# Attention before a feed-forward block: the small products put into 64x64 tiles of the array

## The chip, the core and the metric

One core of a Trainium2 chip runs the whole program. The metric is the device time of one execution in microseconds (us), and the median over several executions is compared. TensorE (PE) does the matrix products and has a separate record for its weight loads (PEld); VectorE (DVE), ScalarE (ACT) and GpSimd (POOL) do the rest; the SyncE queue (SP) issues all transfers.

## The reference, cut to what matters

```
attn:  B, H, S, D = 8, 8, 576, 64     scores = q k^T / 8
       heads 0..3 (local):    key allowed where 0 <= query - key < 32
       heads 4..7 (strided):  key allowed where key <= query and key % 32 == query % 32
       softmax over the allowed keys, times v
x = attn_out as (B*S, H*D) = (4608, 512)
h = x @ w_in                          (512 -> 2048)
out = (h * sigmoid(1.702 h)) @ w_out  (2048 -> 512)
```

All inputs and the output are float32.

## The kernel before, in words

The 4608 tokens go through the feed-forward part (FFN) in 12 groups of G = 384. A group takes 16 steps, one for each 128 columns of the hidden layer. A step does 12 products into the bank `h` (`ffn1`), the activation (`act`), and two steps later (LAG = 2) 9 products into three output banks `o` (`ffn2`). These products are of float32r tiles: each operand is kept as a high and a low part and three of the four cross products are added. A float32r product shows as one matmul record.

The attention is cut into units, listed by `_pairs()`; `p` numbers them. A unit always holds two query blocks (U = 2) of four heads, thus eight score matrices (HU = 8). A local unit has two blocks of 96 queries by 128 keys (QL, KL; 32 keys lie before the block). A strided unit has two blocks in which 6 or 5 of the 32 residues are laid one behind the other: 108 or 90 queries by as many keys (RES), of which only the blocks of 18 by 18 on the diagonal are allowed. There are 24 local and 24 strided units.

For a unit, `scores` computes the eight matrices in plain float32, which the trace shows as two matmul records for each product. Head dimension 64 fills half the rows of the array, and two heads lie on the two halves of the partitions (index j), so their products use rows 0 to 63 and 64 to 127 and write two banks. `maxima` adds the mask and finds the row maxima (DVE), `softmax` does eight exponentials with sums (ACT), two small DVE operations and a scaling on POOL, `transpose` turns the probabilities in 32x32 blocks (DVE), and `values` multiplies by v: the stationary operand is 64 columns of v, the outputs of the two heads go to partitions 0 to 63 and 64 to 127 of one bank `a`. ACT and DVE then split the result into the high and low parts of the FFN's input (`xh..`, `xl..`).

The first n0 units (10 before) are done ahead of the FFN in a loop of their own (line 559). There the mask is added by a bf16 product into the score bank, the probabilities are turned on TensorE (`turn_pr`, tile `t`) and fetched by DVE (`fetch_pt`). One pass of that loop issues, in this order: the scores of unit i+1, the transfer of q and k for unit i+3, the scaling of unit i-1, the exponentials of unit i, the products with v of unit i-2, the load of v for unit i, a weight load, and one beat of the weights' preparation (`weigh`: rebuilding float32 from two words and splitting it, on ACT and DVE; three beats make one of 16 weight tiles). The remaining 38 units are spread over the FFN steps: `due` gives the step in which a unit's probabilities are turned; in the step after it, its products with v and the scores of a unit two later are put between `ffn1` and `ffn2` (lines 641 to 650). The order of the TensorE instructions is kept as written.

Of the kernel before, what the change touches and what calls it, by code (L numbers as in the profile page):

```python
# [9 lines left out]
F32 = mybir.dt.float32  # L10
# [64 lines left out]
def attn_ffn(ctx, tc, qk, vs, w_in, w_out, masks, ident, out):  # L75
# [48 lines left out]
    def load_qk(p):  # L124
        if p < len(pairs) and p not in qks:
            qks[p] = st4([P, 2, 2, U, P], F32, f"qk_{p}")
            for g in (slice(0, 1), slice(1, 2)) if p == 0 else (slice(0, 2),):
                sync.dma_start(out=qks[p][:, :, g], in_=qk[p][:, :, g])

    def load_v(p):  # L130
        if p < len(pairs) and p not in vts:
            vts[p] = io.tile([P, U, HEADS, D], F32, tag="v", name=f"v_{p}", bufs=2)
            sync.dma_start(out=vts[p], in_=vs[p])

# [4 lines left out]
    masks_sb = const.tile([P, 4, P], BF16, name="masks_sb")  # L139
# [12 lines left out]
    prs = [const.tile([P, HU, P], F32, name=f"pr_{i}") for i in range(AHEAD)]  # L152
    pts = {
        "l": const.tile([P, HU, QL], F32, name="pt_l"),
        "s": const.tile([P, HU, P], F32, name="pt_s"),
    }
# [3 lines left out]
    def geom(p):  # L160

        kind, b, c = pairs[p]
        if kind == "l" and c == 0:
            m = masks_sb[:QL, 0:U].rearrange("p u n -> p (u n)")
            return QL, KL, m.unsqueeze(1).broadcast_to([QL, 2, U * KL])
        n, nk, i = (QL, KL, 1) if kind == "l" else (RES[c] * NPOS, RES[c] * NPOS, 2)
        return n, nk, masks_sb[:n, i, :nk].unsqueeze(1).broadcast_to([n, 2 * U, nk])

    def scores(p):

        nq, nk, mask = geom(p)
        t = qks[p]
# [3 lines left out]
        if onto:  # L176
            for sp in sps:
                matmul(
                    sp[:nq, : 2 * U * nk].rearrange("p (a n) -> p a n", a=n),
                    lhsT=masks_sb[:nq, 3, :nq], rhs=mask, start=True, stop=False,  # L180
                )
# [12 lines left out]
        banks[p] = sps  # L194

    def maxima(p):


        nq, nk, mask = geom(p)
        sps, pr, n = banks.pop(p), prs[p % AHEAD], mask.shape[1]  # L200
        nmax = nmaxs[p] = small.tile([P, HU], F32, tag="nmax", name=f"nmax_{p}")
        if p < n0:
            for j in range(2):
                vector.tensor_reduce(
                    out=nmax[:nq, j * 2 * U : (j + 1) * 2 * U],
                    in_=sps[j][:nq, : 2 * U * nk].rearrange("p (h n) -> p h n", n=nk),
                    axis=AX.X, op=ALU.max, negate=True,
                )
            vector.tensor_scalar_mul(out=nmax[:nq], in0=nmax[:nq], scalar1=SCALE)
            exps[p] = [  # L210
                (sps[i // (2 * U)][:nq, i % (2 * U) * nk : (i % (2 * U) + 1) * nk], SCALE)
# [3 lines left out]
        for j in range(2):  # L215
            o = pr[:nq, j * 2 * U : (j + 1) * 2 * U, :nk]
            if n == 2:
                o = o.rearrange("p (g u) n -> p g (u n)", g=2)
            vector.scalar_tensor_tensor(
                out=o, in0=sps[j][:nq, : 2 * U * nk].rearrange("p (a n) -> p a n", a=n),  # L220
# [3 lines left out]
            out=nmax[:nq], in_=pr[:nq, :, :nk], axis=AX.X, op=ALU.max, negate=True  # L224
        )
        exps[p] = [(pr[:nq, i, :nk], 1.0) for i in range(HU)]

    def softmax(p):

        nq, nk, _ = geom(p)  # L230
        nmax, pr = nmaxs.pop(p), prs[p % AHEAD]
        ssum = small.tile([P, HU], F32, tag="ssum", name=f"ssum_{p}")
        for i, (x, scale) in enumerate(exps.pop(p)):
            scalar.activation(
                pr[:nq, i, :nk], x, AF.Exp,
                bias=nmax[:nq, i : i + 1], scale=scale,
                accum_out=ssum[:nq, i : i + 1],
# [4 lines left out]
        vector.tensor_scalar_add(out=rinv[:nq], in0=ssum[:nq], scalar1=1e-9)  # L242
        vector.reciprocal(out=rinv[:nq], in_=rinv[:nq])
        gpsimd.tensor_tensor(
            out=pr[:nq, :, :nk],
            in0=pr[:nq, :, :nk],
            in1=rinv[:nq].unsqueeze(2).broadcast_to([nq, HU, nk]),
# [3 lines left out]
    def transpose(p):  # L251


        nq, nk, _ = geom(p)
        kind, pr = pairs[p][0], prs[p % AHEAD]
        pt = pts[kind]
        for qb in range(-(-nq // BL)):
            for kb in (qb, qb + 1) if kind == "l" else range(max(qb - 1, 0), qb + 1):
                i, o = slice(qb * BL, (qb + 1) * BL), slice(kb * BL, (kb + 1) * BL)
                vector.transpose(out=pt[o, :, i], in_=pr[i, :, o])  # L260

    def turn_pr(p):

        nq, nk, _ = geom(p)
        for i in range(HU):
            n = i % (2 * U)
            transposed(
                first[2][i // (2 * U)][:nk, n * nq : (n + 1) * nq], prs[p % AHEAD][:nq, i, :nk],
                ident_sb[:nq, :nq],
            )  # L270

    def fetch_pt(p):
        nq, nk, _ = geom(p)
        for j, t in enumerate(first[2]):
            vector.tensor_copy(
                out=pts[pairs[p][0]][:nk, j * 2 * U : (j + 1) * 2 * U, :nq],
                in_=t[:nk, : 2 * U * nq].rearrange("p (h n) -> p h n", h=2 * U),
            )
# [4 lines left out]
    def part(kind, j):  # L283
        if (kind, j) not in xs:
            xs[kind, j] = [
                xp.tile([P, 2, G], F32R, tag=f"x{s}_{kind}", name=f"x{s}{kind}_{j}",
                        bufs=2 if kind == "l" else 3)
# [4 lines left out]
    def values(p):  # L292

        kind, b, c = pairs[p]
        nq, nk, _ = geom(p)
        v, pt = vts[p], pts[kind]
        ops = first_a[p % 2 if p < n0 - 3 else 0] if p < n0 else bank(f"a_{p}")
        for u in range(U):
            for g in range(2):
                for j in range(2):  # L300
                    i = g * U + u
                    matmul(
                        ops[j * D : (j + 1) * D, i * nq : (i + 1) * nq],
                        lhsT=v[:nk, u, 2 * g + j, :],
                        rhs=pt[:nk, j * 2 * U + i, :nq],
                        start=True,
                        stop=True,
                    )
        parts = []
        if kind == "l":  # L310
            j, o = divmod((NL * b + c) * QL, G)
            src = ops[:, : 2 * U * nq].rearrange("p (g n) -> p g n", g=2)
            parts.append([src] + [x[:, :, o : o + U * QL] for x in part("l", j)])
        else:
            n, r0 = U * RES[c], R0[c]
            src = ops[:, : 2 * U * nq].rearrange("p (g r t) -> p g t r", g=2, r=n)
            t0 = 0
            while t0 < NPOS:
# [4 lines left out]
                    [src[:, :, t0:t1]] + [x[:, :, o : o + t1 - t0, r0 : r0 + n] for x in xv]  # L323
# [335 lines left out]
def _layout(q, k, v, w_in, w_out):  # L659
    hl = H // 2  # L660
    pad = np.zeros((B, hl, STRIDE, D), np.float32)
    kp, vp = (np.concatenate([pad, x[:, :hl]], axis=2) for x in (k, v))

    def strided(x, b, c):
        y = x[b, hl:].reshape(hl, NPOS, STRIDE, D)[:, :, R0[c] : R0[c] + RES[c]]
        return y.transpose(0, 2, 1, 3).reshape(hl, RES[c] * NPOS, D)

    pairs = _pairs()[0]

    qk = np.zeros((len(pairs), 2, D, 2, 2, U, P), np.float32)  # L670
    vs = np.zeros((len(pairs), P, U, HEADS, D), np.float32)
    for p, (kind, b, c0) in enumerate(pairs):
        for u in range(U):
            c = c0 + u
            if kind == "l":
                i = slice(c * QL, (c + 1) * QL)
                j = slice(c * QL, c * QL + KL)
                x = [q[b, :hl, i], kp[b, :, j], vp[b, :, j]]
            else:
                x = [strided(y, b, c) for y in (q, k, v)]  # L680
            vs[p, : x[2].shape[1], u] = x[2].transpose(1, 0, 2)
            for e, y in enumerate(x[:2]):
                n = y.shape[1]
                qk[p, :, :, e, :, u, :n] = y.reshape(2, 2, n, D).transpose(1, 3, 0, 2)
    qk = qk.reshape(len(pairs), P, 2, 2, U, P)

# [4 lines left out]
    return qk, vs, wi, wo  # L691


def _masks():
    import ml_dtypes

    m = np.full((P, 4, P), NEG, ml_dtypes.bfloat16)
    qi, ki = np.arange(QL)[:, None], np.arange(KL)[None, :] - STRIDE
    rel = qi - ki
    ok = (rel >= 0) & (rel < STRIDE)  # L700
    m[:QL, 0][ok & (ki >= 0)] = 0.0
    m[:QL, 1][ok] = 0.0
    i = np.arange(QS)
    ok = (i[:, None] // NPOS == i[None, :] // NPOS) & (i[:, None] >= i[None, :])
    m[:QS, 2, :QS][ok] = 0.0
    m[:, 3] = np.eye(P)
# [27 lines left out]
```

## Time and profile before

| | |
|---|---|
| median of 3 runs | 938.94 us (938.4 to 941.64) |
| profiled execution | 940.96 us, of which its span is 939.2 us |
| granted TensorE clock, mean of the span | 0.993 of 2.4 GHz |
| PE busy | 924.2 us in 5674 matmul records |
| DVE, ACT, POOL busy | 520.5, 407.7, 85.7 us |

The span runs from the first to the last instruction of the program on the core; 1.76 us of the profiled execution lie around it. A busy time is a sum of records, and records of TensorE overlap, so the share of an engine says only whether it ever pauses. What a piece of work costs on TensorE is better read from the starts of successive records: the time from the start of one block to the start of the next. The line number is L108 throughout, because a helper there records every operation; pieces are told apart by the names of their tiles (`s`, `u` scores; `t` turned probabilities; `a` products with v; `h`, `o` FFN).

### The profile page before, as it was taken

To read this page: it belongs to the slowest core of one execution; us is meant where nothing else is said; L and a number is where in the kernel's file an instruction comes from. 1 tells how busy PE (TensorE), PEld (TensorE's weight loads), DVE (VectorE), ACT (ScalarE), POOL (GpSimd) and SP (SyncE) were. 2 spreads that over 40 slices of the span, in tenths; PEclk is the share of its full clock that TensorE was granted. 3 is DMA by queue.
4 is the path that set the end of the run, shared out by engine and by line. 5 is a ranking of instruction groups with operands and counts; after the bars stand their busy time and mean duration, and the time that the engine had idled before them with its cause. 6 is when DMAs were issued, how large, how long until landed. Compare 5 with 4: busy or idle time off the path is not lost.

```text
span 939.2 us, 14695 instructions
## 1 busy us (share of the span) xinstructions
PE 924.2 (98%) x5674; PEld 813.2 (87%) x5674; DVE 520.5 (55%) x1000; ACT 407.7 (43%) x1289; POOL 85.7 (9%) x56
## 2 busy tenths in 40 slices
PE   8799999999999999999999999999999999999998
PEld 5589888888888888888888888898888888888997
DVE  4787564676666554626757665544656655422322
ACT  6997563434344443325343443333344444222221
POOL 3310000011001100101010100000010101000000
PEclk7999999999999999999999999999999999999999
DMA  7894020222122111103212121102211210000000
GB/s 268 304 343 171 1 90 28 75 68 68 51 75 57 56 35 67 35 0 102 57 45 81 55 68 45 36 21 68 65 37 56 80 46 12 34 1 1 34 1 34
DMA packets 24373, 65.10 MB, mean 69 GB/s; under 512 B 2672, under 2 KB 3440, under 8 KB 24304
## 3 DMA queue, kind: packets, MB, share of 16 engines
q1 hardware_dynamic: 24304, 64.17, 20.3%
q8 instruction: 44, 0.72, 0.3%
q14 instruction: 25, 0.20, 0.1%
HBM read 54.72 MB, written 9.44 MB: 68 GB/s over the span
## 4 chain that ended last, share of the span: by engine, by line
PE 95%; DMA 2%; DVE 1%; ACT 1%; issue 0%; SPq 0%; ACTq 0%
PE o L108 44%; PE h L108 43%; PE s L108 4%; PE a L108 4%; DMA qk<-qk 2%; ACT pr L108 1%; PE u L108 1%; PE t L108 0%; DVE w L108 0%; SPq L108 0%; ACT raw L108 0%; DVE raw L108 0%; DVE nmax L108 0%; DVE pt_l L108 0%; DVE pt_s L108 0%
## 5 line engine op out<-in xcount | busy, mean ns | idle before, releaser
L108 PE MATMUL o<-w,gh 128*128 128x512 f32 x1152 | 308.0, 398 | 0.0
L108 PEld LDWEIGHTS o<-w,gh 128*128 128x128 f32 x1152 | 210.9, 187 | 40.3
L108 PE MATMUL h<-xhl,w 128*128 128x384 f32 x768 | 229.1, 339 | 0.4 <-DVE w L108 0.4
L108 PE MATMUL h<-xhs,w 128*128 128x384 f32 x768 | 226.6, 335 | 0.0
L108 DVE SCALAR_TENSOR_TENSOR g<-g,h 128x384 f32<-128x384 f32 x192 | 106.4, 554 | 194.6 <-ACT g L108 193.7
L108 ACT ACTIVATE g<-h 128x384 f32<-128x384 f32 x192 | 93.5, 487 | 245.0 <-PE h L108 177.5
L108 PE MATMUL o<-w,gl 128*128 128x512 f32 x576 | 169.5, 395 | 0.0
L108 DVE TENSOR_TENSOR gl<-g,gh 128x384 fp32r<-128x384 f32 x192 | 125.9, 656 | 73.5 <-ACT gh L108 72.8
L108 ACT ACTIVATE pr<-pr,nmax 96x128 f32<-96x128 f32 (+2 forms) x304 | 114.2, 378 | 113.1 <-DVE nmax L108 109.6
L108 ACT CAST gh<-g 128x384 fp32r<-128x384 f32 x192 | 98.8, 514 | 130.4 <-DVE g L108 130.1
L108 PEld LDWEIGHTS h<-xhl,w 128*128 128x128 f32 x768 | 141.9, 188 | 9.5 <-DVE w L108 0.7
L108 POOL TENSOR_TENSOR pr<-pr,rinv 96x1024 f32<-96x1024 f32 (+2 forms) x48 | 82.1, 1710 | 707.1 <-DVE rinv L108 630.7
L108 PEld LDWEIGHTS h<-xhs,w 128*128 128x128 f32 x768 | 141.4, 188 | 0.1
L108 PEld LDWEIGHTS o<-w,gl 128*128 128x128 f32 x576 | 107.9, 187 | 26.5
L108 PE MATMUL h<-xll,w 128*128 128x384 f32 x384 | 129.4, 337 | 0.0
L108 PE MATMUL h<-xls,w 128*128 128x384 f32 x384 | 128.3, 334 | 0.0
L108 PEld LDWEIGHTS h<-xll,w 128*128 128x128 f32 x384 | 72.1, 188 | 8.7
L108 PEld LDWEIGHTS h<-xls,w 128*128 128x128 f32 x384 | 72.1, 188 | 0.0
L108 DVE TENSOR_SCALAR rinv<-ssum 96x8 f32<-96x8 f32 (+2 forms) x48 | 8.0, 167 | 96.2 <-ACT pr L108 96.2
L108 ACT ACTIVATION_READ_ACCUMULATOR pr<-pr,nmax 96x1 f32 (+2 forms) x304 | 57.1, 188 | 0.0
L108 DVE STREAM_TRANSPOSE pt_l<-pr 32x256 f32<-32x256 f32 x120 | 52.1, 434 | 3.7 <-POOL pr L108 2.3
L108 PEld LDWEIGHTS s<-qk 64*96 64x96 f32 (+2 forms) x688 | 37.4, 166 | 9.8 <-issue 3.3
(55 smaller groups left out, 555.7 us busy)
## 6 DMA issues: line engine op xcount, KB each, us to landing
qk<-qk SPq DMA_DIRECT2D x47, 512.0 KB, 4.1
v<-vs SPq DMA_DIRECT2D x48, 256.0 KB, 2.8
out<-out SPq DMA_DIRECT2D x36, 256.0 KB, 2.3
raw<-w_in SPq DMA_DIRECT2D x16, 512.0 KB, 5.4
raw<-w_out SPq DMA_DIRECT2D x16, 512.0 KB, 6.3
qk<-qk SPq DMA_DIRECT2D x2, 256.0 KB, 3.3
masks_sb<-masks SPq DMA_DIRECT2D x1, 128.0 KB, 2.2
ident_sb<-ident SPq DMA_DIRECT2D x1, 64.0 KB, 5.1
```

The costliest lines, as they stand in the source:

```text
L108: ins = call(*args, **kw)
```

## The change

Local units become four blocks of 64 queries by 96 keys (QB, KB). Blocks are numbered u and g; block g = 0 goes to output partitions 0 to 63 and g = 1 to 64 to 127, so that one unit covers 256 tokens. There are 18 local units instead of 24. `scores` does 16 products for a unit instead of 8, each with 64 stationary columns; with the head on the rows (j) and the block on the columns (g), four successive products use the four 64x64 quarters of the array. Local `values` does 16 products of 64 columns instead of 8 of 96.

Strided units hold 12 residue places in four blocks of 3 (NB = 54 queries by 54 keys), used as 12, 10 and 10. Their scores are 16 products of 64 stationary columns (10 of them padding) by 54 keys. Their products with v stay 8 for a unit, with both blocks of a pair in one block-diagonal matrix of 118 rows and 108 columns. The number of strided units stays 24.

The units of the loop ahead of the FFN become 9 (2 local, 3 strided, then strided, local, strided, strided); 15 local and 18 strided units are spread over the FFN steps instead of 20 and 18. Every group of rows has all 128 partitions now; the free sizes of scores, exponentials and scaling become 96 (local) and 54 (strided) for each of eight matrices instead of 128 and 108 or 90. Transposes on DVE are 8 for a local unit (6 before) and 6 for a strided one (7 or 5 before). A local unit's q and k take 576 KB and its v 384 KB, a strided unit's 452 KB and 236 KB (512 KB and 256 KB for all units before). The input tiles of the local part have three buffers instead of two, since a unit can reach into the next group. The masks and the host's layout follow the new shapes.

```diff
-QL = 96
-KL = 128
-NL = S // QL
-RES = (6, 6, 5, 5, 5, 5)
-R0 = (0, 6, 12, 17, 22, 27)
-QS = 6 * NPOS
+QB = 64
+KB = QB + STRIDE
+RB = 3
+NB = RB * NPOS
 U = 2
+LT = U * 2 * QB
+NP = B * S // LT
+RES = 4 * RB
+NR = (12, 10, 10)
+R0 = (0, 12, 22)
+QW = (U * 2 * QB, U * (NB + QB))
+KW = (U * (KB + QB), U * 2 * NB)
+QKW = tuple(2 * (a + b) for a, b in zip(QW, KW))
...
     def strided(b):
-        return [("s", b, c) for c in range(0, len(RES), U)]
+        return [("s", b, c) for c in range(len(NR))]
 
     def local(j):
-        n = G // QL
-        return [("l", i // NL, i % NL) for i in range(j * n, (j + 1) * n, U)]
+        return [("l", i, 0) for i in range(-(-j * G // LT), -(-(j + 1) * G // LT))]
...
     def load_qk(p):
         if p < len(pairs) and p not in qks:
-            qks[p] = st4([P, 2, 2, U, P], F32, f"qk_{p}")
-            for g in (slice(0, 1), slice(1, 2)) if p == 0 else (slice(0, 2),):
-                sync.dma_start(out=qks[p][:, :, g], in_=qk[p][:, :, g])
+            kind, a, c = pairs[p]
+            src, n = (lqk[a], QKW[0]) if kind == "l" else (sqk[a * len(NR) + c], QKW[1])
+            qks[p] = st4([P, QKW[0]], F32, f"qk_{p}")
+            for i in (slice(0, n // 2), slice(n // 2, n)) if p == 0 else (slice(0, n),):
+                sync.dma_start(out=qks[p][:, i], in_=src[:, i])
...
+    def operands(p, rows, h, u, g):
+
+        x, kind = qks[p], pairs[p][0] == "s"
+        base = h * QKW[kind] // 2
+        q = base + u * QW[kind] // U + g * (QB, NB)[kind]
+        k = base + QW[kind] + u * KW[kind] // U + g * (QB, NB)[kind]
+        return x[rows, q : q + QB], x[rows, k : k + (KB, NB)[kind]]
...
-        for g in range(2):
+        for h in range(2):
             for u in range(U):
-                for j in range(2):
-                    rows = slice(j * D, (j + 1) * D)
-                    i = g * U + u
-                    matmul(
-                        sps[j][:nq, i * nk : (i + 1) * nk],
-                        lhsT=t[rows, 0, g, u, :nq],
-                        rhs=t[rows, 1, g, u, :nk],
-                        start=not onto,
-                        stop=not onto or i == 2 * U - 1,
-                    )
+                i = h * U + u
+                for g in range(2):
+                    for j in range(2):
+                        q, k = operands(p, slice(j * D, (j + 1) * D), h, u, g)
+                        matmul(
+                            sps[j][g * QB : (g + 1) * QB, i * nk : (i + 1) * nk],
+                            lhsT=q,
+                            rhs=k,
+                            start=not onto,
+                            stop=not onto or i == 2 * U - 1,
+                        )
...
-        for qb in range(-(-nq // BL)):
-            for kb in (qb, qb + 1) if kind == "l" else range(max(qb - 1, 0), qb + 1):
-                i, o = slice(qb * BL, (qb + 1) * BL), slice(kb * BL, (kb + 1) * BL)
-                vector.transpose(out=pt[o, :, i], in_=pr[i, :, o])
+        for g in range(2):
+            for qb in range(QB // BL):
+                for kb in (qb, qb + 1) if kind == "l" else range(qb + 1):
+                    i = slice(g * QB + qb * BL, g * QB + (qb + 1) * BL)
+                    o = slice(kb * BL, (kb + 1) * BL)
+                    at = slice(g * QB + kb * BL, g * QB + (kb + 1) * BL) if kind == "s" else o
+                    vector.transpose(out=pt[at, :, i], in_=pr[i, :, o])
...
         if kind == "l":
...
+            for u in range(U):
+                for g in range(2):
+                    for h in range(2):
+                        for j in range(2):
+                            o = (h * U + u) * 2 * QB + g * QB
+                            matmul(
+                                ops[j * D : (j + 1) * D, o : o + QB],
+                                lhsT=v[:KB, U * u + g, 2 * h + j, :],
+                                rhs=pt[:KB, j * 2 * U + h * U + u, g * QB : (g + 1) * QB],
+                                start=True,
+                                stop=True,
+                            )
...
         else:
...
+            for u in range(U):
+                for h in range(2):
+                    for j in range(2):
+                        x = pt[: QB + NB, j * 2 * U + h * U + u, :]
+                        matmul(
+                            out4[j * D : (j + 1) * D, h, :, u, :],
+                            lhsT=v[: QB + NB, u, 2 * h + j, :],
+                            rhs=x.rearrange("p (g n) -> p g n", g=2)[:, :, :NB],
+                            start=True,
+                            stop=True,
+                        )
```

## Rows read from the trace of the kernel before

**Rows 1.** The page's first part: busy time, share of the span and records of each engine.

```profile
PE 924.2 (98%) x5674; PEld 813.2 (87%) x5674; DVE 520.5 (55%) x1000; ACT 407.7 (43%) x1289; POOL 85.7 (9%) x56
```

**Rows 2.** Busy time of each engine by stretch (start and end, length, then busy time and number of records for PE, PEld, DVE, ACT, POOL; granted clock, DMA share, GB/s).

```profile
25.00:45.00 20.00, 14.86 (x185) 11.10 (x184) 17.16 (x44) 20.00 (x94) 7.69 (x5) 0.99 0.91 326
60.00:80.00 20.00, 20.00 (x102) 18.02 (x101) 17.02 (x23) 20.00 (x26) 0.00 (x0) 1.00 0.78 292
94.00:800.00 706.00, 706.00 (x4348) 625.09 (x4347) 413.27 (x794) 296.27 (x987) 65.67 (x38) 1.00 0.16 53
800.00:939.20 139.20, 135.25 (x695) 120.45 (x693) 41.78 (x76) 33.59 (x67) 0.00 (x0) 1.00 0.05 18
```

**Rows 3.** TensorE's matmuls in order of time (start, length from the first start to the last end, output and input tiles, stationary rows and columns, moving rows and columns, number of records): a strided unit of 90, a local unit, products with v of a strided unit of 108, scores of a strided unit of 108, and a step without attention.

```profile
302.00 0.34 PE L108 MATMUL h<-xhs,w 128*128 128x384 f32 x1
302.27 0.84 PE L108 MATMUL a<-pt_s,v 90*64 90x90 f32 x16
303.04 0.88 PE L108 MATMUL s<-qk 64*90 64x90 f32 x16
303.85 0.50 PE L108 MATMUL o<-w,gh 128*128 128x512 f32 x1
...
316.38 0.34 PE L108 MATMUL h<-xhs,w 128*128 128x384 f32 x1
316.65 0.88 PE L108 MATMUL a<-pt_l,v 128*64 128x96 f32 x16
317.46 1.12 PE L108 MATMUL s<-qk 64*96 64x128 f32 x16
318.51 0.50 PE L108 MATMUL o<-w,gh 128*128 128x512 f32 x1
...
196.19 0.96 PE L108 MATMUL a<-pt_s,v 108*64 108x108 f32 x16
197.08 0.88 PE L108 MATMUL s<-qk 64*90 64x90 f32 x16
...
240.54 1.01 PE L108 MATMUL s<-qk 64*108 64x108 f32 x16
241.48 0.50 PE L108 MATMUL o<-w,gh 128*128 128x512 f32 x1
...
307.98 0.34 PE L108 MATMUL h<-xhs,w 128*128 128x384 f32 x1
308.16 0.39 PE L108 MATMUL o<-w,gh 128*128 128x512 f32 x1
```

**Rows 4.** Groups of instructions by form: the scores and the products with v over the whole span (busy time, mean ns of one record | idle before).

```profile
L108 PE MATMUL s<-qk 64*96 64x128 f32 x368 | 26.6, 285 | 0.0
...
L108 PE MATMUL a<-pt_l,v 128*64 128x96 f32 x384 | 22.5, 263 | 0.0
...
L108 PE MATMUL a<-pt_s,v 90*64 90x90 f32 x256 | 14.1, 248 | 0.3
...
L108 PE MATMUL s<-qk 64*90 64x90 f32 x208 | 11.4, 249 | 0.0
...
L108 PE MATMUL a<-pt_s,v 108*64 108x108 f32 x128 | 8.1, 263 | 0.0
...
L108 PE MATMUL s<-qk 64*108 64x108 f32 x112 | 7.8, 285 | 0.0
```

**Rows 5.** The same timeline in narrow windows, so that a row counts only the records that have started by the window's end: local scores in the window 317.4 to 317.6; products with v of a strided unit of 108 in the windows 26.1 to 26.28 and 26.1 to 26.42; the turning products `t` on the whole array in 27.3 to 28.

```profile
317.46 0.35 PE L108 MATMUL s<-qk 64*96 64x128 f32 x2
...
26.15 0.31 PE L108 MATMUL a<-pt_s,v 108*64 108x108 f32 x1
...
26.15 0.40 PE L108 MATMUL a<-pt_s,v 108*64 108x108 f32 x2
...
27.32 0.82 PE L108 MATMUL t<-ident_sb,pr 90*90 90x90 f32 x8
27.98 0.38 PE L108 MATMUL s<-masks_sb 96*96 96x512 bf16 x1
```

**Rows 6.** Weight loads of the scores and of the products with v, by tile (duration in ns: least, median, most; first and last start; forms).

```profile
L108 PEld LDWEIGHTS s<-qk x688: 151/160/297, 4.5 to 783.5; 64*96 64x96 f32 x92, 64*90 64x90 f32 x52, 64*108 64x108 f32 x28
...
L108 PEld LDWEIGHTS a<-pt_l,v x384: 132/137/230, 18.1 to 831.8; 128*64 128x64 f32 x192
```

**Rows 7.** ACT in the loop ahead of the FFN, in order of time: successive exponentials of a strided unit of 90 and of a local unit.

```profile
22.27 0.32 ACT L108 ACTIVATE pr<-u,nmax 90x90 f32<-90x90 f32 x1
22.58 0.32 ACT L108 ACTIVATE pr<-u,nmax 90x90 f32<-90x90 f32 x1
...
42.69 0.53 ACT L108 ACTIVATE pr<-s,nmax 96x128 f32<-96x128 f32 x1
43.03 0.53 ACT L108 ACTIVATE pr<-s,nmax 96x128 f32<-96x128 f32 x1
```

**Rows 8.** The end of that loop: a piece of the chain of work that ended last (start, length, what), TensorE's scores of the tenth unit with the idle time before them, and the sizes of the units' transfers (KB each, median us from issue to landing).

```profile
34.19 9.89 DMA qk<-qk
...
44.12 1.22 PE L108 MATMUL u<-qk 64*90 64x90 f32 x16 [2.63 <-DMA qk<-qk]
...
qk<-qk SPq DMA_DIRECT2D x47, 512.0 KB, 4.1
v<-vs SPq DMA_DIRECT2D x48, 256.0 KB, 2.8
```

More of the change, by code (lines that the diff above doesn't have):

```diff
@@ L149, in attn_ffn @@
     first_a = [bank(f"a{j}") for j in range(2)]
[L152 to L156, printed above, removed]
+    prs = [const.tile([P, HU, KB], F32, name=f"pr_{i}") for i in range(AHEAD)]
+    pts = {k: const.tile([P, HU, P], F32, name=f"pt_{k}") for k in "ls"}
     for x in prs + list(pts.values()):
@@ L160, in geom @@
     def geom(p):
[L162 to L167, printed above, removed]
+        kind, a, _ = pairs[p]
+        if kind == "s":
+            m = masks_sb[:, MASK_S : MASK_S + NB]
+            return NB, m.unsqueeze(1).broadcast_to([P, 2 * U, NB])
+        begins = [i for i in range(2 * U) if (2 * U * a + i) % (S // QB) == 0]
+        if not begins:
+            m = masks_sb[:, KB : 2 * KB]
+            return KB, m.unsqueeze(1).broadcast_to([P, 2 * U, KB])
+        at = (0, 2, 3, 1)[begins[0]] * KB
+        m = masks_sb[:, at : at + U * KB]
+        return KB, m.unsqueeze(1).broadcast_to([P, 2, U * KB])
+    def operands(p, rows, h, u, g):
[4 more added lines that the diff above has]
+        return x[rows, q : q + QB], x[rows, k : k + (KB, NB)[kind]]
     def scores(p):
-        nq, nk, mask = geom(p)
-        t = qks[p]
+        nk, mask = geom(p)
         onto = p < n0
@@ L223, in maxima @@
         vector.tensor_reduce(
[L224 removed]
+            out=nmax, in_=pr[:, :, :nk], axis=AX.X, op=ALU.max, negate=True
         )
[L226 removed]
+        exps[p] = [(pr[:, i, :nk], 1.0) for i in range(HU)]
     def softmax(p):
[L230 removed]
+        nk, _ = geom(p)
         nmax, pr = nmaxs.pop(p), prs[p % AHEAD]
@@ L309, in values @@
         parts = []
         if kind == "l":
-            j, o = divmod((NL * b + c) * QL, G)
-            src = ops[:, : 2 * U * nq].rearrange("p (g n) -> p g n", g=2)
-            parts.append([src] + [x[:, :, o : o + U * QL] for x in part("l", j)])
-        else:
-            n, r0 = U * RES[c], R0[c]
-            src = ops[:, : 2 * U * nq].rearrange("p (g r t) -> p g t r", g=2, r=n)
+            v = v.rearrange("p (b h d) -> p b h d", b=2 * U, h=HEADS)
+            for u in range(U):
+                for g in range(2):
+                    for h in range(2):
[8 more added lines that the diff above has]
+                            )
@@ new lines, in values @@
+            src = ops.rearrange("p (g n) -> p g n", g=2)
+            t0 = 0
+            while t0 < LT:
+                j, o = divmod(LT * b + t0, G)
+                t1 = min(LT, t0 + G - o)
+                parts.append([src[:, :, t0:t1]] + [x[:, :, o : o + t1 - t0] for x in part("l", j)])
+                t0 = t1
+        else:
+            v = v[:, : U * HEADS * D].rearrange("p (u h d) -> p u h d", u=U, h=HEADS)
+            out4 = ops[:, : 8 * NB].rearrange("p (h g u n) -> p h g u n", h=2, g=2, u=U)
+            for u in range(U):
[9 more added lines that the diff above has]
+                        )
+            n, r0 = NR[c], R0[c]
+            src = ops[:, : 8 * NB].rearrange("p (g r t) -> p g t r", g=2, r=RES)
@@ L662, in _layout @@
     kp, vp = (np.concatenate([pad, x[:, :hl]], axis=2) for x in (k, v))
[L664 to L684, printed above, removed]
@@ L685, in _layout @@
-    qk = qk.reshape(len(pairs), P, 2, 2, U, P)
+    nb = S // QB
+    lqk = np.zeros((NP, 2, D, 2, QKW[0] // 2), np.float32)
+    lv = np.zeros((NP, KB, 2 * U, HEADS, D), np.float32)
+    for i in range(NP):
+        for m in range(2 * U):
+            b, n = divmod(2 * U * i + m, nb)
+            u, g = divmod(m, 2)
+            rows = q[b, :hl, n * QB : (n + 1) * QB]
+            keys = kp[b, :, n * QB : n * QB + KB]
+            at = u * 2 * QB + g * QB
+            lqk[i, :, :, :, at : at + QB] = rows.reshape(2, 2, QB, D).transpose(1, 3, 0, 2)
+            at = QW[0] + u * (KB + QB) + g * QB
+            skip = STRIDE if g and not n else 0
+            lqk[i, :, :, :, at + skip : at + KB] = keys[:, skip:].reshape(
+                2, 2, KB - skip, D
+            ).transpose(1, 3, 0, 2)
+            lv[i, :, m] = vp[b, :, n * QB : n * QB + KB].transpose(1, 0, 2)
@@ new lines, in _layout @@
+    ns = B * len(NR)
+    sqk = np.zeros((ns, 2, D, 2, QKW[1] // 2), np.float32)
+    sv = np.zeros((ns, QB + NB, U, HEADS, D), np.float32)
+    for i in range(ns):
+        b, c = divmod(i, len(NR))
+        for m in range(2 * U):
+            g, u = divmod(m, U)
+            r0, r1 = R0[c] + RB * m, R0[c] + min(RB * (m + 1), NR[c])
+            n = (r1 - r0) * NPOS
+            x = [
+                y[b, hl:].reshape(hl, NPOS, STRIDE, D)[:, :, r0:r1].transpose(0, 2, 1, 3).reshape(hl, n, D)
+                for y in (q, k, v)
+            ]
+            at = u * (NB + QB) + g * NB
+            sqk[i, :, :, :, at : at + n] = x[0].reshape(2, 2, n, D).transpose(1, 3, 0, 2)
+            at = QW[1] + u * 2 * NB + g * NB
+            sqk[i, :, :, :, at : at + n] = x[1].reshape(2, 2, n, D).transpose(1, 3, 0, 2)
+            sv[i, g * QB : g * QB + n, u] = x[2].transpose(1, 0, 2)
@@ L688, in _layout @@
+    lqk, sqk = (x.reshape(len(x), P, -1) for x in (lqk, sqk))
+    lv, sv = (x.reshape(*x.shape[:2], -1) for x in (lv, sv))
     wi = w_in.reshape(NC, P, NF, P).transpose(2, 1, 0, 3).reshape(NF, P, DM)
```

115 lines of the change are left out of this document (57 added, 58 removed).

## Prediction

> **What bounds the kernel now.** I read the page's first part, then the stretches, then TensorE's timeline around the attention blocks, and last the loop ahead of the FFN. The reader should see first that TensorE is busy for 98% of the span and every other engine for 55% or less [rows 1]. The stretches say where this means a limit: from 94 to 800 us TensorE is busy for 706.0 of 706.0 us at a granted clock of 1.00, while DVE is busy for 59%, ACT for 42% and DMA moves 53 GB/s [rows 2]. There a microsecond less on TensorE is a microsecond less of time, and what DVE, ACT, POOL and the transfers do is hidden. From 25 to 45 us it is different: ACT is busy for 20.00 of 20.00 us and TensorE for 14.86, so the loop ahead of the FFN goes at ACT's pace; from 60 to 80 us both are full [rows 2]. The last stretch has only FFN work and stays as it is.
>
> **What an attention block costs.** I take costs from starts, since records overlap. A step without attention goes from its last `h` to its first `o` in 0.18 us (307.98 to 308.16) [rows 3]. With a unit the switch from `h` to `a` takes 0.27, so 0.09 more. The blocks are then: products with v 0.81 (local, 96 columns), 0.77 (90), 0.89 (108); scores 1.05 (local, 128 columns), 0.81 (90), 0.94 (108) [rows 3]. Each block has 8 products in 16 records; the counts agree (384 records for 24 local units, 256 and 128 for the strided ones) [rows 4].
>
> Now split these. Eight products `t` on the whole array start 0.66 us apart in sum, 82 ns each; 90 columns passed twice at 2.4 GHz are 75 ns [rows 5]. So a float32 record passes its columns twice. Sixteen records of 90 columns would need 1.2 us one by one, and the blocks of 90 take 0.77 and 0.81: two records run at once, in the scores on two halves of the rows, in the products with v on two halves of the columns. Eight pairs at two passes are 0.853 us for 128 columns, 0.72 for 108, 0.64 for 96, 0.60 for 90. What is left is the price of a block whatever its size: 0.17 for `a` (0.81 - 0.64, 0.77 - 0.60, 0.89 - 0.72) and 0.20 to 0.22 for `s`.
>
> Two rows tell in which order the two records of a product go. Local scores show two records within 0.35 us [rows 5], about one record's length. At 26.15 a product started alone: one record, and with the second the row is 0.40 us long; less the 0.26 of a record [rows 4], the second began 0.14 us later [rows 5]. So the second record of a product waits for its first, on the same part of the array, and a neighbour fills the rest. With four parts there are four neighbours to draw on.
>
> **The change, part by part.**
>
> Local scores: 16 products, 32 records of 96 columns. If four run at once, 8 groups of 80 ns are 0.64, with 0.20 for the block 0.84. The second records of one pair overlap the first of the next, which leaves half a group open at the ends; I take 0.90.
>
> Strided scores: 32 records of 54 columns, 8 groups of 45 ns, 0.36 + 0.20 = 0.56. No block in the trace is that short. The weights must follow: records of loads are 137 ns for 64 columns against a median of 160 where most have 96 [rows 6], 0.72 ns a column, thus an estimate of 46 ns for 64, as long as the group itself. The upper bound is today's block of 90, 0.81. I take 0.70, the middle.
>
> Local products with v: 32 records of 64 columns, still two at once: 16 pairs of 53 ns are 0.85, with 0.17 it is 1.02; the same load of weights has to fit, so I take 1.05. Per unit this is dearer than 0.81: it covers 256 tokens instead of 192, but with shorter columns and more pairs. Strided products with v have 108 columns in all units now: 0.89.
>
> The sum over the units spread in the FFN: before, 20 x (0.09 + 0.81 + 1.05) = 39.0, 12 x (0.09 + 0.77 + 0.81) = 20.0, 6 x (0.09 + 0.89 + 0.94) = 11.5, together 70.5 us. After, 15 x (0.09 + 1.05 + 0.90) = 30.6 and 18 x (0.09 + 0.89 + 0.70) = 30.2, together 60.8. That is 9.7 us less. With the lower values (1.02, 0.84, 0.56) it is 57.0, 13.5 less.
>
> DVE, ACT and POOL: transposes go from 222 to 228 in this part; mask, maxima, exponentials and scaling shrink. ACT's copies of local results are sometimes two instead of one. All of it lies beside a TensorE that is full while DVE is idle for 41% and ACT for 58% of the stretch [rows 2]; I cost it at nothing. Were that cover gone, six transposes more would be under 3 us. The transfers are hidden too, at 53 GB/s.
>
> The loop ahead of the FFN: ten units become nine. Successive exponentials start 0.31 us apart for 90 columns and 0.34 for 128 [rows 7], so 96 columns cost about 0.315 and 54 about 0.28. Before: 32 x 0.34 + 16 x 0.325 + 32 x 0.31 = 26.0 us of ACT; after: 24 x 0.315 + 48 x 0.28 = 21.0. ACT sets the pace, so 5.0 us go. Against it stands one beat of the weights' preparation, which the missing pass no longer does and the first FFN steps must, about 1 us. I take 4.0 less. The lower bound is nothing: the first two units' transfers grow from 768 to 960 KB each, 384 KB in sum, at 326 GB/s 1.2 us on a DMA that is 91% busy there [rows 2], and ACT may then wait for the weights behind them. The upper bound is 7.6: the tenth unit's scores waited 2.63 us for q and k, whose transfer took 9.89 us behind four weight transfers issued before it [rows 8]; the ninth unit's are asked for one pass earlier, ahead of those weights, so this wait can go as well. What is late next is then the weights themselves.
>
> Sum against the profiled execution: 939.2 - 9.7 - 4.0 = 925.5 of span, 927.3 with the 1.76 around it. The median of the runs lies 2.0 below the profiled execution, so I forecast 925 for the median.
>
> **A rule that speaks against it.** The closest mean spacing of record starts in the trace is 48 ns (0.77 us for 16) [rows 3]; the change needs 26 ns in local scores and 18 in strided ones. The Trainium skill (TensorEngine Tiling (Array Packing), section Instruction Overhead) says that each matmul has about 60 cycles of overhead on trn2 and that no tiling factor should be taken from a dimension that is already small. Sixty cycles at 2.4 GHz are 25 ns, so 32 records would be 0.80 and both score blocks 1.00, an estimate from that page that would leave about 3 us of the 9.7. No row shows which holds.
>
> **Rivals.**
>
> *Only two records at once.* Four parts are offered, but the order of records or the weight loads keep two busy. Scores are then 16 x 80 + 200 = 1.48 us local and 16 x 45 + 200 = 0.92 strided; the sum is 15 x 2.62 + 18 x 1.90 = 73.5, 3.0 more than before, and with 4.0 from the loop the time is 938. For it: nothing in the trace shows more than two at once. Against it: rows and columns each overlap by themselves at full rate, so neither the reading of operands nor the weights of one half hold up the other half. This is the case in which the change does not do what it says.
>
> *A floor on the spacing of starts.* With the starts no closer than 24 ns, half of what is seen now, both score blocks are 32 x 24 + 200 = 0.97; the sum is 15 x 2.11 + 18 x 1.95 = 66.8, 3.7 less, and the time 931.
>
> *The loop gives nothing,* because the larger local transfers or the weights set its pace: 929.
>
> *Slower: changing the half of the columns drains the array.* A change of tile shape costs 0.17 to 0.22 us in every block. If within the scores each change between g = 0 and g = 1 cost 0.10, eight of them in 33 units would add 26 us: 951. It decides from 52 ns a change on (13.7 us over 33 x 8). Against it: products with v change the half of the columns at every product today, at 48 ns a record.
>
> **How the numbers follow.** Chances: forecast 0.55 (925, its own range 918 to 929), loop without gain 0.12 (929), floor 0.10 (931), two at once 0.15 (938), drain 0.06 (951), the rest 0.02. The range runs from 918 (938.9 - 13.5 - 7.6) to 939, to take in two at once. The runs of the kernel before differ by 3.2 us, so 0.5%, 4.7 us, is about what a measurement can tell from no change. Under 934.2: 0.76, the first three with a little taken off; within: 0.17; over 943.6: 0.07.
>
> **What would show it.** In a step with attention, local scores take 0.85 to 0.95 us and strided ones 0.56 to 0.81 from their first start to the first `o`; narrow windows count four records within one record's length. At 1.48 and 0.92 two at once is right; at about 1.0 for both the floor is; far more, the drain. Local products with v should take 1.05. The first `o` of the FFN comes 4 us earlier; if not, the wait ahead of ACT's exponentials or weight beats names the late transfer. The prediction is wrong if TensorE stops being busy throughout in the long middle stretch: then a wait on `pr`, `pt` or `v` that nothing shows now would be the cause.

## The result, and the profile after

The changed kernel is slower: a median of 946.76 us (945.31 to 947.53, 4 runs) against 939.14 us (938.40 to 941.64, 4 runs) for the kernel before, a ratio of 1.0075 with a 95% interval of 1.0052 to 1.0097. The forecast was 925, with a range from 918 to 939. The profiled execution has a span of 945.7 us, 6.5 more than before.

The busy times of the page, the stretches 25 to 45, 45 to 70 and 94 to 800 us, and a piece of the chain of work that ended last (start, length, what), all of the changed kernel:

```profile
PE 913.9 (97%) x6432; PEld 806.6 (85%) x6432; DVE 476.1 (50%) x986; ACT 380.6 (40%) x1193; POOL 53.0 (6%) x50
```

```profile
25.00:45.00 20.00, 11.29 (x206) 9.07 (x202) 13.89 (x41) 13.44 (x67) 4.14 (x4) 0.82 0.60 189
45.00:70.00 25.00, 16.85 (x150) 14.65 (x152) 10.32 (x25) 11.26 (x43) 1.88 (x3) 0.73 0.61 186
94.00:800.00 706.00, 705.96 (x5014) 626.67 (x5013) 382.12 (x794) 285.67 (x926) 39.75 (x33) 1.00 0.16 52
```

```profile
26.49 10.14 DMA v<-sv
36.77 1.72 PE a L116 x16
38.50 15.25 DMA v<-sv
53.89 1.72 PE a L116 x16
55.63 14.05 DMA v<-sv
69.81 0.96 PE a L116 x16
71.65 11.10 DMA raw<-w_out
```

The long stretch is as full as before [rows 2]. The loop ahead of the FFN is another kernel: between 25 and 45 us ACT is busy for 13.44 us where it was full, the DMA share is 0.60 where it was 0.91 [rows 2], and the granted clock is 0.82. The chain names what sets the pace now: three loads of v for strided units, 10.14, 15.25 and 14.05 us long, fill 39.4 us of it. Before, a load of v took 2.4 to 9.1 us, in the median 2.8 [rows 8]. The last row shows a transfer of weights that is late behind them.

The first `o` of the FFN divides the span into the loop (with the start) and the rest. That division places the gain and the loss in every kernel of this study but one, e9_late_raw3, whose rest holds a loss of its own (below):

| kernel | span | first `o` | from there to the end |
|---|---|---|---|
| before | 939.2 | 59.31 | 879.9 |
| changed | 945.7 | 76.65 | 869.0 |
| e1_pad128 | 929.6 | 61.92 | 867.7 |
| e2_before118 | 954.6 | 74.70 | 879.9 |
| e3_two_at_once | 940.6 | 62.59 | 878.0 |
| e4_before112 | 937.2 | 57.34 | 879.9 |
| e5_late_qk / e5b_late_qk | 923.2 / 928.7 | 55.55 / 61.10 | 867.7 / 867.6 |
| e6_raw3 | 924.3 | 56.16 | 868.1 |
| e8_118_spread | 927.9 | 60.17 | 867.7 |
| e9_late_raw3 | 927.4 | 54.91 | 872.5 |
| e10_before116 | 944.2 | 64.35 | 879.9 |
| e11_split112 | 934.0 | 65.49 | 868.5 |

From the changed kernel's first `o` on, the part with the spread units gained 10.8 us; the loop lost 17.3. TensorE's timeline shows the gain, in two steps of the FFN (strided, then local), and in narrow windows that count only the records started by their end: strided scores in 215.45 to 215.59 and to 215.65, local scores in 266.95 to 267.12.

```profile
214.61 0.96 PE L116 MATMUL a<-pt_s,v 118*64 118x108 f32 x16
215.50 0.69 PE L116 MATMUL s<-qk 64*64 64x54 f32 x32
216.12 0.50 PE L116 MATMUL o<-w,gh 128*128 128x512 f32 x1
...
303.31 1.15 PE L116 MATMUL a<-pt_l,v 96*64 96x64 f32 x32
304.39 0.89 PE L116 MATMUL s<-qk 64*64 64x96 f32 x32
305.21 0.50 PE L116 MATMUL o<-w,gh 128*128 128x512 f32 x1
...
215.50 0.28 PE L116 MATMUL s<-qk 64*64 64x54 f32 x4
...
215.50 0.34 PE L116 MATMUL s<-qk 64*64 64x54 f32 x8
...
267.00 0.31 PE L116 MATMUL s<-qk 64*64 64x96 f32 x4
```

From start to start, strided scores take 0.62 us (216.12 - 215.50), local scores 0.82, products with v 0.89 and 1.08. Four records lie within 0.28 and 0.31 us, where before it were two within 0.35 [rows 5]. Taken over all spread units, what a step with a unit costs above one without is 71.0 us in sum before and 59.2 after. That is 11.8 less, a microsecond more than the rest of the span gained. Most of that microsecond is a wait: after its first `o` the changed kernel still waits for weights (0.52 us at 84.08, 0.21 at 88.78). e1_pad128 has no such wait there, and its rest is 12.2 shorter than before.

TensorE's timeline in the loop shows the loss (in brackets the idle time before a row and what ended it), and under it SP's issues of v:

```profile
36.77 1.71 PE L116 MATMUL a<-pt_s,v 118*64 118x108 f32 x16 [3.86 <-DMA v<-sv]
45.78 1.71 PE L116 MATMUL a<-pt_s,v 118*64 118x108 f32 x16 [4.05 <-DMA v<-sv]
53.89 1.71 PE L116 MATMUL a<-pt_s,v 118*64 118x108 f32 x16 [3.83 <-DMA v<-sv]
62.47 1.79 PE L116 MATMUL a<-pt_l,v 96*64 96x64 f32 x32 [3.07 <-DMA v<-lv]
```

```profile
38.50 0.26 SPq L116 DMA_DIRECT2D v<-sv  x1
47.52 0.33 SPq L116 DMA_DIRECT2D v<-lv  x1
55.63 8.91 SPq L116 DMA_DIRECT2D v<-sv  x2
```

Four products with v wait 3 to 4 us each for a load, 14.8 us in sum. One of these loads has 96 rows and is a local unit's: it was issued at 47.52 and the product could start at 62.47, 15 us later. Its semaphore rose 14 times by 55.72 us, and for the last two times only at 61.39 and 62.33. What the loads are short of is seen in two windows of a microsecond in which TensorE and ACT stand still (columns as in the stretches above; the last two are the DMA share and GB/s):

```profile
60.00:61.00 1.00, 0.00 (x0) 0.00 (x0) 0.20 (x1) 0.00 (x0) 0.60 (x1) 1.00 0.13 48
61.00:62.00 1.00, 0.00 (x0) 0.00 (x0) 0.00 (x0) 0.00 (x0) 0.31 (x1) 1.00 0.12 49
```

A share of 0.125 is two of the 16 DMA engines. The v of a strided unit is now 118 rows, and 118 = 2 x 59. At 48 GB/s its 236 KB need 5.0 us by themselves; in the trace the 118 packets of such a load, 2048 bytes each, are spread over 5.4 to 7.2 us in this stretch, and the load issued at 38.50 has its first packet only at 45.77. In the two windows shown no packet of a strided v is in flight. Two packets at a time are, of 4096 and 4608 bytes, which are rows of local v or of weights and rows of a local unit's q and k: these two engines still have to move their part of the other transfers.

### The profile page after: what moved, and what is told of

Same layout as the page of the kernel before. It is cut to its first block, busy times and chain, and to the rows that moved or that the text cites. A ratio compares the mean times of both kernels' runs of the same rounds, so it can differ in the third digit from the quotient of the medians.

```text
span 945.7 us, 16069 instructions
## 1 busy us (share of the span) xinstructions
PE 913.9 (97%) x6432; PEld 806.6 (85%) x6432; DVE 476.1 (50%) x986; ACT 380.6 (40%) x1193; POOL 53.0 (6%) x50
## 4 chain that ended last, share of the span: by engine, by line
PE 92%; DMA 7%; DVE 0%; issue 0%; SPq 0%; ACT 0%; DVEq 0%; ACTq 0%
PE o L116 43%; PE h L116 41%; PE a L116 4%; DMA v<-sv 4%; PE s L116 3%; DMA raw<-w_out 1%; DMA qk<-sqk 1%; DMA qk<-lqk 1%; PE u L116 0%; PE t L116 0%; SPq L116 0%; ACT raw L116 0%; DVE raw L116 0%; DVE w L116 0%; DVE out L116 0%
## 5 line engine op out<-in xcount | busy, mean ns | idle before, releaser
L116 PEld LDWEIGHTS h<-xhl,w 128*128 128x128 f32 x768 | 142.3, 188 | 12.2 <-DVE w L116 2.3
L116 DVE TENSOR_TENSOR gl<-g,gh 128x384 fp32r<-128x384 f32 x192 | 112.0, 583 | 77.6 <-ACT gh L116 76.1
L116 ACT ACTIVATE pr<-pr,nmax 128x54 f32<-128x54 f32 (+1 forms) x264 | 90.3, 344 | 87.6 <-DVE nmax L116 84.6
L116 POOL TENSOR_TENSOR pr<-pr,rinv 128x432 f32<-128x432 f32 (+1 forms) x42 | 49.6, 1182 | 734.5 <-DVE rinv L116 728.0
L116 DVE STREAM_TRANSPOSE pt_s<-pr 32x256 f32<-32x256 f32 x108 | 47.1, 436 | 9.5 <-POOL pr L116 8.0
L116 ACT ACTIVATION_READ_ACCUMULATOR pr<-pr,nmax 128x1 f32 x264 | 49.4, 187 | 0.0
L116 PE MATMUL a<-pt_s,v 118*64 118x108 f32 x384 | 25.3, 278 | 13.8 <-DMA v<-sv 12.2
```

Of the source, the lines that this page charges most:

```text
L116: ins = call(*args, **kw)
```

## The experiments

The theory: a transfer of 118 rows is moved by two of the DMA engines, and the six loads of strided v in the loop cost the time. The first rival: a longer loop has another cause, such as the larger local transfers or the new order of units. The second question was whether the scores gain because four products run at once.

**Rows alone, in the changed kernel.** e1_pad128 gives strided v 128 rows again, ten of them zeros; 256 KB instead of 236.

```diff
-                sync.dma_start(out=vts[p][: QB + NB, :n], in_=sv[a * len(NR) + c])
+                sync.dma_start(out=vts[p][:, :n], in_=sv[a * len(NR) + c])
...
-    sv = np.zeros((ns, QB + NB, U, HEADS, D), np.float32)
+    sv = np.zeros((ns, P, U, HEADS, D), np.float32)
```

> The changed kernel with one edit: v of a strided unit is stored and loaded with 128 rows instead of 118 (ten rows of zeros more, which no product reads). Theory (118 rows are spread over few DMA engines, since 118 = 2 x 59, and these loads hold up the loop ahead of the FFN): the loads no longer show as waits of the products with v, the first FFN output comes before 57 us, and the time falls by 15 to 24 us to 923 to 932, since the spread part already saves about 12 us. Rival A (the loop is late because the local units' transfers are larger or the q and k rows are longer or shorter): more bytes are loaded here, so the time stays at 945 or above. Rival B (the four quarters of the array cost clock or order in the loop): stays at 945.

Measured: 931.93 us (931.42 to 932.97), 0.9922 of the kernel before (0.9905 to 0.9939), and 14.8 below the changed kernel with more bytes moved. That is at the edge of what was expected (15 to 24 below), and the first `o` comes at 61.92, later than the 57 expected. From 25 to 45 us ACT is nearly full again, as before the change; what is left of the loss shows in the loop's one long wait for a load of v, on TensorE's timeline and in the chain (first the stretch, with the columns as above):

```profile
25.00:45.00 20.00, 14.44 (x242) 11.20 (x240) 18.85 (x54) 19.57 (x98) 5.11 (x5) 1.00 0.98 325
```

```profile
47.08 1.97 PE L116 MATMUL a<-pt_l,v 96*64 96x64 f32 x32 [4.32 <-DMA v<-lv]
```

```profile
37.55 9.40 DMA v<-lv
```

**Rows alone, in the kernel before.** e2_before118 loads 118 of the 128 rows of strided v; the units use 108 or 90 of them. e10_before116 loads 116 (4 x 29), e4_before112 loads 112 (16 x 7).

```diff
-            sync.dma_start(out=vts[p], in_=vs[p])
+            n = 118 if pairs[p][0] == "s" else P
+            sync.dma_start(out=vts[p][:n], in_=vs[p][:n])
```

> The kernel before with one edit: v of a strided unit is loaded with 118 rows instead of 128; rows past 108 are not read. Theory: slower by 10 to 20 us though fewer bytes move, with waits of the products with v for that load in the first 80 us. Rivals A and B: no change, within 0.3%.

> The kernel before with v of a strided unit loaded with 116 rows (4 x 29). Theory (a transfer is spread over the largest number of DMA engines, at most 16, that divides its rows: 118 over 2, 116 over 4, 112 over 16): between the 939 of 112 or 128 rows and the 956 of 118, with stretches in which 4 of 16 engines, a share of 0.25, are busy; an estimate is 1 to 8 us slower than before. Rival (a row number that 16 does not divide falls to 2 engines): 956.

> The kernel before with v of a strided unit loaded with 112 rows (16 x 7) instead of 128. Theory (the number of rows decides over how many DMA engines a transfer is spread): no change, within 0.3%. Rival (any transfer of fewer than 128 rows is slow): slower by about as much as the load of 118 rows.

Measured: 956.19 us with 118 rows (ratio 1.0176, 1.0156 to 1.0195), 945.99 with 116 and 938.99 with 112, against 939.05 to 939.91 for the kernel before. Fewer bytes make it slower, and it is the rows' divisor that decides. One microsecond of e2_before118 and one of e10_before116, and of e2_before118 the chain:

```profile
54.00:55.00 1.00, 0.00 (x0) 0.00 (x0) 0.00 (x0) 1.00 (x8) 0.00 (x0) 0.50 0.13 51
```

```profile
50.00:51.00 1.00, 1.00 (x24) 0.82 (x20) 0.68 (x2) 0.00 (x0) 0.00 (x0) 1.00 0.25 96
```

```profile
18.62 8.29 DMA v<-vs
28.77 12.90 DMA v<-vs
50.76 12.32 DMA v<-vs
```

The share is 0.13 with 118 rows and 0.25, four of 16, with 116. With 116 rows the longest wait of TensorE in the loop is for q and k (3.02 us at 49.42), which are late together with v: from 48 to 51 us four packets are in flight at a time, of v and of larger transfers. In e2_before118 everything from the first `o` on takes 879.9 us as before; the whole loss, 15.4 us, lies in the loop. The rival falls: with the old sizes and the old order of units the loop loses about as much. e10_before116 and e4_before112 are single runs, but they stand 6 us above and level with the kernel before, whose runs lie within 4 us of each other.

**Where the 118 rows hurt.** e8_118_spread is e1_pad128 with 118 rows again, but only in the units spread over the FFN.

```diff
-                sync.dma_start(out=vts[p][:, :n], in_=sv[a * len(NR) + c])
+                m = P if p < n0 else QB + NB
+                sync.dma_start(out=vts[p][:m, :n], in_=sv[a * len(NR) + c, :m])
```

> e1 with the 118-row loads of v kept for the 18 strided units of the spread part and 128 rows only for the 6 of the loop. Theory (slow loads are hidden in the spread part, where v is asked for several steps ahead): the same time as e1 within 0.3%, and the six loads of the loop alone cost the 14.8 us between the changed kernel and e1. Rival (slow loads cost wherever they are): a part of the 14.8 us comes back, up to three quarters.

Measured: 929.64 us in one run, within 0.3% of e1_pad128. Beside the FFN the slow loads cost nothing that one run can tell; those of the six strided units in the loop cost the 15 us.

**The same rows in two transfers.** e11_split112 leaves the host's layout and moves 112 rows and then 6.

```diff
-                sync.dma_start(out=vts[p][: QB + NB, :n], in_=sv[a * len(NR) + c])
+                for i in (slice(0, 112), slice(112, QB + NB)):
+                    sync.dma_start(out=vts[p][i, :n], in_=sv[a * len(NR) + c, i])
```

> The changed kernel with v of a strided unit still of 118 rows, loaded as two transfers of 112 and 6 rows. Theory: the time of e1, 928 to 933. Rival (it is the address or size of these rows that is slow, not their number): 945 or above.

Measured: 935.76 us in one run, 11.0 below the changed kernel but above the 928 to 933 expected. The wait for strided v is nearly gone (0.23 us at 37.25); one wait for a local unit's v is left, longer than in e1_pad128, and both kinds of v still stand in the chain:

```profile
51.04 1.98 PE L116 MATMUL a<-pt_l,v 96*64 96x64 f32 x32 [7.19 <-DMA v<-lv]
```

```profile
29.45 7.67 DMA v<-sv
38.84 12.06 DMA v<-lv
```

So the 112 rows take back most of the loss. Why the loads are later than with 128 rows, the six rows or this execution, is open.

**Four at once.** e3_two_at_once is e1_pad128 with the block g in the outermost loop of the scores, so that successive products alternate between two heads on one half of the columns.

```diff
-        for h in range(2):
-            for u in range(U):
-                i = h * U + u
-                for g in range(2):
+        for g in range(2):
+            for h in range(2):
+                for u in range(U):
+                    i = h * U + u
```

> e1 with the loop over the column half g outermost in the scores, so that successive products change only the half of the rows: the same products in another order. Theory (four records run at once): a block of local scores goes from 0.82 to about 16 x 82 + 180 ns = 1.50 us and one of strided scores from 0.62 to about 16 x 58 + 150 ns = 1.08 us, in sum 15 x 0.68 + 18 x 0.46 = 18 us more than e1. Rival (the gain in the scores comes only from shorter columns and fewer units, two at once): the same time as e1.

Measured: 942.43 us in one run, a span 11.0 above that of e1_pad128, with 878.0 instead of 867.7 from the first `o` on. The blocks are, local and strided:

```profile
253.57 1.27 PE L116 MATMUL s<-qk 64*64 64x96 f32 x32
254.78 0.97 PE L116 MATMUL o<-w,gh 128*128 128x512 f32 x3
...
201.28 0.96 PE L116 MATMUL s<-qk 64*64 64x54 f32 x32
202.17 0.50 PE L116 MATMUL o<-w,gh 128*128 128x512 f32 x1
```

From start to start 1.21 and 0.89 where the changed order has 0.82 and 0.62: 15 x 0.39 + 18 x 0.27 = 10.7 us, which is the 10.3 that the rest of the span lost. So the gain hangs on neighbours that use different quarters. The expectation of 18 us more was too high. It held that this order runs two at once throughout (1.50 and 1.08). The starts of the records show four pairs alone, then four groups of four, then four pairs alone: 12 steps, where two at once would need 16 and the changed order has 8. At 82 ns a step, and 58 for strided units, 12 steps and the 0.20 of a block are 1.18 and 0.90, against the 1.21 and 0.89 measured. The groups of four must be records of the other half of the columns begun among those of the first; that is read from the order of the products, as a record does not name its quarter. How TensorE chooses among them is not settled by this run.

**What is left in the loop.** In e1_pad128 the late load is the local unit's v. SP's issues show what it queues behind, four weight transfers and the q and k of a unit that is needed only in the FFN:

```profile
33.22 0.44 SPq L116 DMA_DIRECT2D raw<-w_in  x1
33.70 0.42 SPq L116 DMA_DIRECT2D raw<-w_out  x1
34.17 0.43 SPq L116 DMA_DIRECT2D raw<-w_in  x1
34.65 0.75 SPq L116 DMA_DIRECT2D raw<-w_out  x1
35.49 0.59 SPq L116 DMA_DIRECT2D qk<-lqk  x1
37.55 0.33 SPq L116 DMA_DIRECT2D v<-lv  x1
```

All that follow are e1_pad128 with a further edit. e5_late_qk lets the loop load only the q and k that it uses itself, and loads those of the next two units after it; e5b_late_qk is the same kernel, timed over more executions. e6_raw3 takes one of four weight buffers away, so that fewer weights are asked for early. e9_late_raw3 does both.

```diff
-            load_qk(i + 3)
+            if i + 3 < n0:
+                load_qk(i + 3)
...
+    for p in (n0, n0 + 1):
+        load_qk(p)
```

```diff
-RAWB = 4
+RAWB = 3
```

> e1 with only the late load of q and k of the first two spread units. Theory: the 4.3 us wait for v shrinks by the 576 KB that no longer lie ahead of it, 1.8 us at 330 GB/s, and the time by as much.

> e1 with only the weights loaded three tiles ahead instead of four. Theory: the 4.3 us wait for v shrinks by the 1 MB that no longer lies ahead of it, about 3.2 us. Rival: a later wait of ACT for weights takes it back.

> e1 with two edits in the loop ahead of the FFN: q and k of the first two units that belong to the spread part are loaded after the loop, and weights are loaded three tiles ahead instead of four (one weight tile's 1 MB instead of 2 MB is queued in the sixth pass). Theory (what is left of the loss in e1 is the local unit's v, landing 9.4 us after its issue behind 2 MB of weights and 0.6 MB of early q and k): the 4.3 us wait of the products with v goes, TensorE's clock does not fall at 45 us, and the time is 3 to 6 us below e1, 926 to 929. Rival (ACT's work or the weights set the end of the loop anyway): within 1.5 us of e1, with a wait for weights in place of the wait for v.

> The kernel of e5 again, timed over more executions: 128 rows of v, q and k of the first two spread units loaded after the loop. Theory (with both transfer faults gone the loop gives about the 4 us that the prediction took, beside the 12 us of the spread part): 924 to 927, 12 to 15 us under the kernel before. Rival (the single time was a lucky one): 929 to 932, as e1.

Measured: e5_late_qk 925.0 us and e6_raw3 926.13, one run each; e9_late_raw3 928.57 (926.46 to 930.67), ratio 0.9878 (0.9851 to 0.9906); e5b_late_qk 928.39 (926.32 to 930.52), ratio 0.9867 (0.9847 to 0.9887). The two single runs gained more on e1_pad128 than expected (6.9 us where 1.8 was, 5.8 where 3.2 was); e9_late_raw3 is within its 926 to 929. e5b_late_qk falls between its theory (924 to 927) and its rival (929 to 932), so the 925.0, below all of its five runs, was in part luck. TensorE's waits for v are gone in all of them, and the chains show what is late instead, the weights: first e5b_late_qk, then e6_raw3, then e9_late_raw3.

```profile
35.79 6.79 DMA raw<-w_in
```

```profile
51.09 6.17 DMA raw<-w_out
```

```profile
49.83 8.98 DMA raw<-w_out
```

In e9_late_raw3 the loss only moves. Its first `o` is the earliest of all, at 54.91, but then TensorE waits for weights within the FFN, and from there to the end it takes 872.5 us where e1_pad128 takes 867.7:

```profile
62.49 0.45 PE L116 MATMUL h<-xhl,w 128*128 128x384 f32 x1 [1.01 <-ACT w L116]
64.81 0.61 PE L116 MATMUL h<-xhl,w 128*128 128x384 f32 x2 [1.70 <-DVE w L116]
```

The kernel of e5_late_qk reached its first `o` at 55.55 us in one profile and at 61.10 in the other, so one profile of this loop settles no difference under some 5 us. The two versions with several runs can't be told apart; e5b_late_qk keeps the gain in the FFN and takes 1.3% less time than the kernel before and 1.9% less than the changed one.

## Why the prediction was wrong

**The scores and the spread units: right.** The forecast for this part was 70.5 us before and 60.8 after; it is 71.0 and 59.2. Of the four blocks, the products with v came out as forecast (1.05 against 1.08, 0.89 against 0.89). Both score blocks are 0.08 shorter than I took: 0.82 instead of 0.90, and 0.62 instead of 0.70. For the local block the half group left open at the ends did not show; eight groups of 80 ns and 0.20, the lower bound of 0.84, were right. For the strided block the lower bound of 0.56 was not reached: the first four records end 0.28 us after the start and the first eight 0.34, so a group follows after 58 ns rather than the 45 of its columns. Local products with v also start in pairs 58 ns apart, although their 64 columns need 53. A load of 64 weight columns is common to both, and 46 ns was my estimate for it; that it sets the 58 is argued from these rows and was not tried, and a least length of a record on one quarter would fit the two figures as well.

The sum had one misreading beside it that changes no figure: the stretch from 800 us on holds more than FFN work, two products with v at 800.85 and 831.26, and the sum had counted their units.

The rivals of the scores fall. Two at once throughout would have left 1.48 and 0.92, a floor on the starts 0.97 for both, a drain at each change of the half of the columns far more than 0.9. The floor is refuted by the spacing itself: 32 starts in 0.62 us are 19 ns each, and within the block four in 58 ns, 14.6 ns each. The Trainium skill's rule (TensorEngine Tiling (Array Packing), section Instruction Overhead) of some 60 cycles for each matmul, taken as a least spacing of all starts, does not hold across four quarters here: the estimate from it in the prediction made strided scores 1.00, and they took 0.62.

**The loop: the step that failed.** "I take 4.0 less. The lower bound is nothing" became 17.3 us more. The step counted the loop's transfers by their bytes, and by bytes the strided v was the harmless one, 236 KB instead of 256, so no term stood for it. What counts is how the rows divide: 118 rows go over two engines. The part on ACT held: exponentials of 54 columns start 0.28 us apart as taken (27.04 and 27.32 in e1_pad128). But ACT sets the pace only where the loads come in time. With the rows put right by e1_pad128, the loop still reaches its first `o` 2.6 us later than before instead of 4.0 earlier. That part was foreseen in kind: "ACT may then wait for the weights behind them" named a queue in which one transfer is late behind others, though I placed the weights at its end and it was the local unit's v. With q and k asked for later, the first `o` came 3.8 us earlier than before in one execution and 1.8 later in the other; the gain of 4.0 is thus within reach of this loop, but its transfers do not give it every time.

The rule was there to be read: the Trainium skill (DMA: Bandwidth & Descriptors, section Why a DMA increments its semaphore by 16 and not by 1) says that a transfer is spread over the largest number of engines, up to 16, that divides the slowest dimension of both its sides. The runs agree with it at 118 rows (share 0.13, two engines), 116 (0.25, four) and 112, which cost nothing (938.99).

**The sum.** Expected -9.7 in the FFN and -4.0 in the loop; measured -10.8 and +17.3, together the 6.5 us by which the spans differ. The only rival above the range, a drain in the array, looked for the danger on TensorE; it lay in the number of rows of one transfer, which no rival named.

## What to carry to other kernels

Read the number of rows of each transfer that a change touches, not only its KB: take a multiple of 16 (112 cost nothing, 118 cost 17 us), and pad rather than trim. Look at such a transfer where it is exposed: the same 118 rows cost nothing that one run could tell beside a full TensorE, and the whole loss in the loop ahead of it. And where a product fills a quarter of the array, order its neighbours over all four quarters; here that order was worth some 10 us (e3_two_at_once).

## What the runs showed of the hardware

A transfer over two engines is slow for others too. The changed kernel's load of a local unit's v, 96 rows, issued at 47.52, raised its semaphore 16 times: 14 times between 53.47 and 55.72 us, and the last two at 61.39 and 62.33, while the DMA share stood at 0.12. So it needed two engines that were far behind the other 14, and could be used only 15 us after its issue.

The waits cost more than their length. After each idle stretch of 4 us in the loop of the changed kernel, the next strided block of products with v takes 1.71 to 1.72 us where the same kind of block takes 0.96 beside the FFN at a granted clock of 1.00. In the five microseconds that hold the first of them the granted clock is 0.54, close to the lower of the two levels (1.2 of 2.4 GHz):

```profile
35.00:40.00 5.00, 3.23 (x24) 2.69 (x25) 1.83 (x5) 1.33 (x3) 0.91 (x1) 0.54 0.41 137
```

Records of the four quarters start in groups of four within some 20 ns, with 58 ns from group to group in strided scores. Over the whole block that is 19 ns a record, where the closest of the kernel before is 48 [rows 3].
